# Sums of attention weights in one PSUM bank, and new positions for every task of a fused attention and soft mixture-of-experts kernel

## The chip, the cores and the metric

One NeuronCore of a Trainium2 chip runs the whole program. The metric is the device time of one execution in microseconds; lower is better. All data is float32 in and out.

## The reference, cut to what matters

```
# q, k, v: (8 batches, 8 heads, 576 positions, 64)
q_rot, k_rot = (rotate(q), rotate(k))              # halves mixed by cos and sin of the position
scores = scale * np.matmul(q_rot, k_rot.transpose(0, 1, 3, 2))
scores = scores - np.max(scores, axis=-1, keepdims=True)
attn = np.exp(scores)
attn = attn / (np.sum(attn, axis=-1, keepdims=True) + 1e-09)
x = np.matmul(attn, v)                             # -> (4608 tokens, 512)

logits = x @ phi                                   # phi: (512, 32 slots)
d = softmax of logits over all tokens ; slot_input = d.T @ x
slot_out[e] = np.maximum(slot_input[e] @ w1[e], 0.0) @ w2[e]     # 8 experts, 4 slots each
c = softmax of logits over the slots ; out = c @ slot_out
```

Both softmaxes subtract a maximum and add 1e-9 to the sum that they divide by. The four lines on the experts are cut; the first six are as they stand in the reference.

## The kernel before, in words

Two heads make a pair; there are 32 pairs, four to a batch. A pair keeps head 0 in partitions 0 to 63 and head 1 in 64 to 127, with the position (576, worked on as two halves of 288) along the free axis. After the last pair comes a tail: the slots, the experts' two layers with 64 weight tiles of 512 KB, and the output.

What one pair goes through, by task name:

- `load0`, `load1`: q and k by DMA into one of two buffers `x_in`. `spin0`, `spin1`: GpSimd multiplies them by cos and sin in place, four pieces of 128x288 each. `join`: VectorE adds the two products. `high0`, `high1`: ScalarE casts to float16. `low`: VectorE takes what the cast lost; both go into `hl`, and `x_in` is free for the next pair but one.
- `m00` to `m31` and `m_rem`: nine times TensorE makes a block of the scores in plain float16 and VectorE reduces it to a negated maximum `nm` (L175, L183). `m_min`, `m_turn`, `m_half`, `m_rows`: the maxima are joined, transposed, scaled and sent by DMA into a row `peak`.
- `t0` to `t8`: TensorE makes the scores, keys along the partitions, with three float16 products and a fourth that subtracts the maximum (16 matmuls, L220); ScalarE writes exp of them to SBUF (L221). Two of `t0` to `t7` share a tile `a_t` of 128x1152, of which there are four; `t8` writes `a_rem`. The sum over the keys is thus a sum over partitions and over nine pieces.
- `av0` to `av8`: TensorE multiplies the weights by v (8 instructions, L236) into one PSUM tile; `o_out` copies it to `xt` on ScalarE (L244).
- `add1`, `add2`, `add3`: VectorE adds the four tiles `a_t` into `c_t`: two additions of 128x1152 (L253) and one of 128x576 (L255). `total`: TensorE sums four pieces over the partitions with a matrix `pick` of ones and zeros (16 instructions, L265), each piece in an own 32 columns of the array, the two halves of the positions in two banks. `total_out` copies the sums to SBUF on ScalarE (L270).
- `send`: four DMAs lay the sums out over 96 partitions (`rc`, L276). `recip`: VectorE adds the four and takes the reciprocal (L282, L283). `spread`, `widen`: two steps of DMA through DRAM spread it over all partitions (`rb`, L289, L296). `norm`: GpSimd multiplies `xt` (L299). The last two pairs do this by TensorE and VectorE instead (`sums_turn`, `sums_wide`, `norm_wide`).
- `logits`, `logits_sum`, `natural`, `natural_out`: the pair's part of the logits, and `xt` transposed. After every fourth pair come `stats` and `step`: the running softmax over tokens, `slot_input`, and the softmax over slots.

TensorE writes everything but the products with v into tiles `s_ps` of two banks each, of which there are three, taken in turn. Each engine, and the DMA queue of SyncE (SP), carries out its instructions in the order in which they are written. That order is set by the table `WHEN`: a task's number is its place in a cycle of four units, counted from the pair's own cycle, and all pairs use the same numbers. So a pair's load stands four cycles ahead of its `t0`, and its `natural` nearly three cycles behind. The start, up to the first `t0`, is written out by hand (lines 600 to 660). While pairs run, `weights` loads 25 weight tiles, one in a cycle; `trickle` loads eight more once the buffers of q and k are free.

Of the kernel before, what the change touches and what calls it, by code (L numbers as in the profile page):

```python
# [7 lines left out]
F32 = mybir.dt.float32  # L8
# [39 lines left out]
    "load0": -15.9, "load1": -14.496, "spin0": -13.466, "spin1": -12.4, "join": -9.9, "high0": -9.4817, "high1":  # L48
    -9.0595, "low": -8.0, "m01": -6.5262, "m10": -5.894, "m00": -5.0601, "m11": -4.7, "load_v": -3.85, "m20": -3.771,
    "m21": -3.317, "m30": -2.9, "m31": -2.7, "m_rem": -2.6642, "m_min": -2.49, "m_turn": -1.744, "m_half": -1.667,  # L50
# [4 lines left out]
    "o_out": 4.52, "add3": 4.6009, "total": 5.54, "total_out": 5.55, "send": 5.56, "sums_turn": 6.0, "sums_wide": 6.3,  # L55
    "norm_wide": 6.4, "logits_late": 7.0, "logits_sum_late": 7.05, "recip": 7.294, "natural_late": 7.3, "spread": 7.31,
    "natural_out_late": 7.35, "widen": 7.3768, "norm": 8.706, "logits": 10.54, "logits_sum": 10.579, "stats": 11.3708,
    "natural": 11.52, "natural_out": 11.536,
}
QL, QH, KH, KL = range(4)  # L60
# [3 lines left out]
def attn_softmoe(ctx, tc, qk, v, phi, w1, w2, cs, ident, sel, seg, out):  # L64
# [30 lines left out]
    bits = const.tile([P, 5], F32, name="bits")  # L95
    ones, warm, tiny, fold = bits[:, 0:1], bits[:, 1:2], bits[:, 2:3], bits[:, 3:5]
# [8 lines left out]
    pick = const.tile([P, NS + 1], F32, name="pick")  # L105
    nc.gpsimd.memset(pick, 0.0)
    for h in (0, 1, 2):
        nc.gpsimd.memset(pick[rows[h % 2], h:h + 1], 1.0)

    nc.vector.memset(tiny, 0.0)  # L110
    nc.vector.memset(tiny[0:32], 1e-9)
# [146 lines left out]
    rcs = [const.tile([96, 4, RC], F32, name=f"rc{i}") for i in range(2)]  # L258
# [27 lines left out]
    def spread(p, eng):  # L286
        rr = sg.pop(p)
        rd = dram.tile([2, S], F32, name="r_row")
# [645 lines left out]
```

## Time and profile before

| | |
|---|---|
| median of 3 runs | 613.8 us (610.75 to 618.16) |
| span of the profiled execution | 611.8 us |
| busy: TensorE, VectorE | 532.9 us (87%), 497.0 us (81%) |
| busy: ScalarE, GpSimd | 326.9 us (53%), 315.1 us (52%) |
| DMA | 111.63 MB, 182 GB/s over the span |
| first and last `o_out` | 49.9 and 525.6 us from the span's start |

The span runs from the first to the last instruction of the profiled execution; its own device time is not given apart from it, and the span lies 2.0 us below the median of the runs, within their spread. The pairs take the stretch from 50 to 526 us, the tail the rest.

### The profile page before, as it was taken

The page shows a single profiled execution, that of the slowest core. Times are in us where ns is not written, and L with a number is a line of the kernel's source. Part 1 is how long each engine was busy: PE and PEld are TensorE (multiplying, and loading weights), DVE is VectorE, ACT ScalarE, POOL GpSimd, SP SyncE. Part 2 cuts the span into 40 slices and gives each one's busy share as a digit, 9 for nine tenths or more (in the row PEclk, how much of TensorE's full clock was granted, in tenths as well). Part 3 has the DMA queues.
Part 4 walks back from the last instruction along what each step waited for, and adds up shares of the span by engine and source line. Part 5 has one row for each costly group of instructions (what it writes and reads, how often), then busy time and mean ns, then how long its engine had stood idle before and what let it go on. Part 6 is the DMA issues. An engine that isn't in the chain of part 4 may idle for free.

```text
span 611.8 us, 23277 instructions
## 1 busy us (share of the span) xinstructions
PE 532.9 (87%) x10064; PEld 352.1 (58%) x10064; DVE 497.0 (81%) x729; ACT 326.9 (53%) x647; POOL 315.1 (52%) x308
## 2 busy tenths in 40 slices
PE   3668999998999899989999899898898999799981
PEld 2346666656765566666656565666566666443551
DVE  6879899999998999999998999999899874322341
ACT  2145656665665565656656566565465655324441
POOL 2668498655676566647763857658654000100000
PEclk9679999999999999999999999999899999859996
DMA  7153555555555555555555555455542246649999
GB/s 260 60 195 119 175 174 173 174 174 173 174 173 174 174 174 174 173 175 174 174 173 175 173 174 174 174 174 174 171 141 62 64 130 206 206 142 350 349 376 298
DMA packets 71734, 111.63 MB, mean 182 GB/s; under 512 B 20176, under 2 KB 47568, under 8 KB 71632
## 3 DMA queue, kind: packets, MB, share of 16 engines
q1 hardware_dynamic: 71618, 110.15, 54.5%
q8 instruction: 79, 1.29, 0.9%
q14 instruction: 23, 0.19, 0.1%
q10 hardware_dynamic: 14, 0.00, 0.0%
HBM read 99.93 MB, written 9.58 MB: 179 GB/s over the span
## 4 chain that ended last, share of the span: by engine, by line
PE 35%; DVE 26%; DMA 20%; ACT 6%; SPq 5%; issue 5%; POOL 1%; DVEq 0%; ACTq 0%
PE s_ps L220 8%; PE o_ps L236 8%; DVE nm L175 7%; DMA rc<-s 7%; DMA w_exp<-in_w 6%; DVE c_t L253 6%; DVE hl L153 5%; SPq L276 4%; ACT a_t L221 3%; PE s_ps L265 3%; DMA x_in<-in_qk 3%; PE s_ps L773 3%; DMA v_in<-in_v 2%; DVE c_t L255 2%; PE s_ps L173 2%
## 5 line engine op out<-in xcount | busy, mean ns | idle before, releaser
L140 POOL TENSOR_TENSOR x_in<-x_in,cs_sb 128x288 f32<-128x288 f32 x248 | 264.9, 1101 | 63.0 <-DMA x_in<-in_qk 38.1
L221 ACT ACTIVATE a_t<-s_ps 128x576 f32<-128x576 f32 x256 | 158.9, 649 | 97.8 <-PE s_ps L220 95.9
L175 DVE TENSOR_REDUCE nm<-s_ps 128x2 f32<-128x576 f32 x256 | 187.1, 743 | 15.1 <-PE s_ps L173 14.9
L236 PE MATMUL o_ps<-a_t,v_in 64*64 64x288 f32 x2048 | 172.4, 413 | 1.0 <-ACT xt L244 0.3
L220 PE MATMUL s_ps<-hl 64*64 64x288 f16 x3456 | 155.5, 286 | 16.4 <-DVE nm L175 15.9
L220 PEld LDWEIGHTS <-hl 64*64 64x64 f16 x3456 | 104.4, 107 | 59.9 <-issue 43.8
L299 POOL TENSOR_TENSOR xt<-xt,rb 128x576 f32<-128x576 f32 x30 | 42.8, 1425 | 141.0 <-DMA rb<-r_row 104.1
L173 PE MATMUL s_ps<-hl 64*64 64x288 f16 x1024 | 82.1, 298 | 26.0 <-DVE nm L175 20.5
L220 PE MATMUL s_ps<-peak,lift 64*64 64x288 f16 x1152 | 89.1, 284 | 0.0
L236 PEld LDWEIGHTS o_ps<-a_t,v_in 64*64 64x64 f32 x2048 | 72.9, 133 | 21.0 <-issue 7.3
L173 PEld LDWEIGHTS <-hl 64*64 64x64 f16 x1024 | 45.0, 107 | 49.1 <-issue 37.7
L149 ACT CAST hl<-x_in 128x576 f16<-128x576 f32 (+1 forms) x66 | 40.1, 650 | 33.1 <-DVE x_in L144 30.3
L270 ACT ACTIVATE s<-s_ps,bits 128x576 f32<-128x576 f32 x32 | 23.7, 740 | 58.0 <-PE s_ps L265 26.3
L144 DVE TENSOR_TENSOR x_in<-x_in 128x1152 f32<-128x1152 f32 (+2 forms) x36 | 53.4, 1483 | 0.5 <-POOL x_in L140 0.4
L253 DVE TENSOR_TENSOR c_t<-c_t,a_t 128x1152 f32<-128x1152 f32 x32 | 51.6, 1611 | 0.0
L153 DVE TENSOR_TENSOR hl<-x_in,hl 128x1152 f16<-128x1152 f32 x32 | 49.5, 1546 | 1.8 <-ACT hl L149 1.8
L253 DVE TENSOR_TENSOR c_t<-a_t 128x1152 f32<-128x1152 f32 x32 | 50.6, 1582 | 0.0
L220 PEld LDWEIGHTS <-lift 64*64 64x64 f16 x1152 | 38.1, 108 | 0.6
L265 PE MATMUL s_ps<-c_t,pick 128*32 128x288 f32 x256 | 37.1, 411 | 0.0
L265 PE MATMUL s_ps<-a_rem,pick 128*32 128x288 f32 x128 | 36.9, 411 | 0.0
L265 PE MATMUL s_ps<-a_t,pick 128*32 128x288 f32 x128 | 36.9, 411 | 0.0
L221 ACT ACTIVATE a_rem<-s_ps 128x576 f32<-128x576 f32 x32 | 20.8, 651 | 17.0 <-PE s_ps L220 17.0
(183 smaller groups left out, 597.6 us busy)
## 6 DMA issues: line engine op xcount, KB each, us to landing
x_in<-in_qk SPq DMA_DIRECT2D x62, 576.0 KB
w_exp<-in_w SPq DMA_DIRECT2D x63, 512.0 KB
v_in<-in_v SPq DMA_DIRECT2D x32, 576.0 KB
rb<-r_row SPq DMA_DIRECT2D x60, 144.0 KB
out<-w_exp SPq DMA_DIRECT2D x16, 512.0 KB
rc<-s SPq DMA_DIRECT2D x120, 4.5 KB
x_in<-in_qk SPq DMA_DIRECT2D x4, 288.0 KB
out<-w_exp SPq DMA_DIRECT2D x4, 256.0 KB
```

The costliest lines, as they stand in the source:

```text
L140: eng.tensor_tensor(out=x[:, :, c], in0=x[:, :, c], in1=cs_sb[:, :, c], op=ALU.mult)
L144: nc.vector.tensor_tensor(out=x[:, t, 0, c], in0=x[:, t, 0, c], in1=x[:, t, 1, c], op=ALU.add)
L149: nc.scalar.copy(out=halves[p][:, 1 + t, c], in_=loaded[p][:, t, 0, c])
L153: nc.vector.tensor_tensor(out=hl[:, 0:4:3], in0=x[:, :, 0], in1=hl[:, 1:3], op=ALU.subtract)
L173: nc.tensor.matmul(s[rows[c], h, 0:HC], lhsT=hl[rows[h], QH, at:at + D], rhs=hl[rows[h], KH, half[n]], start=True, stop=True)
L175: nc.vector.tensor_reduce(out=nms[p][:, n, j:8:4], in_=s[:, :, 0:HC], axis=AX.X, op=ALU.max, negate=True)
L220: nc.tensor.matmul(s[rows[h ^ n], n, 0:HC], lhsT=lhs, rhs=rhs, start=(i == 0), stop=(i == 3))
L221: nc.scalar.activation(out=weights_of(p, b).rearrange("p (n x) -> p n x", n=2), in_=s[:, :, 0:HC], func=AF.Exp, scale=SCALE)
L236: nc.tensor.matmul(o[rows[h], n, 0:HC], lhsT=vt[r, b, n], rhs=a[r, half[n]], start=(b == 0), stop=(b == KB - 1))
L253: nc.vector.tensor_tensor(out=c, in0=c if j > 1 else ats[p, 0], in1=a, op=ALU.add)
L265: nc.tensor.matmul(s[32 * i:32 * i + 32, n, 0:HC], lhsT=pick[:, n:n + NS], rhs=m[:, half[n]], start=True, stop=True, tile_position=(0, 32 ...
L299: eng.tensor_tensor(out=xts[p], in0=xts[p], in1=rbs.pop(p), op=ALU.mult)
```

## The change

The weights of `t4` to `t7` are no longer all added on VectorE. `add1` is as before; `add2` now adds only the first half of the third `a_t` (128x576), and `add3` is gone. `total` sums six pieces in place of four, in three rounds that accumulate in PSUM; the two halves of the positions take 32 columns of the array each, so the result fills 288 columns of one bank in place of two times 288. `total_out` then copies 128x288, `send` is two DMAs, `recip` adds two parts, `widen` reads rows of 288 in place of 576. The sums' other readers (`sums_turn`, `sums_wide`, `norm_wide`) follow that layout.

The table of positions has one number for each pair's place in its batch, and a table of its own (`FIRST`) for the first four pairs; the start, the steps after each batch and the last pairs are in tables too, and all tasks are sorted by them. With that the order of nearly all tasks of all engines differs, at the start also of the loads of q, k, v, `ident` and `phi`. The small matrix `fold` is made by one GpSimd addition late in the run instead of four VectorE copies at the start. The last 64 of the 576 positions are transposed as columns 448 to 576 and used from partitions 64 to 127.

```diff
 WHEN = {
-    "load0": -15.9, "load1": -14.496, "spin0": -13.466, "spin1": -12.4, "join": -9.9, "high0": -9.4817, "high1":
...
+    "load0": (-16.4019, -15.2769, -15.1452, -14.3382), "load1": (-14.3952, -13.4352, -13.0199, -13.9565), "spin0":
...
+FIRST = {
+    "load0": (-16.6363, -9.672, -3.3892, -0.9218), "load1": (3.3939, -6.7488, -2.9737, -0.5436), "spin0": (-7.8087,
...
     def add(p, j):
         if j == 1:
             cts[p] = att.tile([P, 2, S], F32, name="c_t")
-        c, a = cts[p], ats[p, j]
-        if j < 3:
-            nc.vector.tensor_tensor(out=c, in0=c if j > 1 else ats[p, 0], in1=a, op=ALU.add)
+            nc.vector.tensor_tensor(out=cts[p], in0=ats[p, 0], in1=ats[p, 1], op=ALU.add)
         else:
-            nc.vector.tensor_tensor(out=c[:, 1], in0=c[:, 1], in1=a[:, 1], op=ALU.add)
+            c = cts[p][:, 0]
+            nc.vector.tensor_tensor(out=c, in0=c, in1=ats[p, 2][:, 0], op=ALU.add)
...
     def total(p):
-        c, r, a = cts.pop(p), rems[p], ats[p, 3]
+        c, a2, a3 = cts.pop(p), ats[p, 2], ats[p, 3]
+        streams = ((c[:, 0], c[:, 1], a2[:, 1]), (a3[:, 0], a3[:, 1], rems[p]))
         sg[p] = s = bank2()
-        for n in range(2):
-            for i, m in enumerate((c[:, 0], c[:, 1], r, a[:, 0])):
-                nc.tensor.matmul(s[32 * i:32 * i + 32, n, 0:HC], lhsT=pick[:, n:n + NS], rhs=m[:, half[n]],
-                                 start=True, stop=True, tile_position=(0, 32 * i))
+        for i in range(3):
+            for k in range(2):
+                for n in range(2):
+                    g = 32 * (n + 2 * k)
+                    nc.tensor.matmul(s[g:g + 32, 0, 0:HC], lhsT=pick[:, 16 * n:16 * n + 32], rhs=streams[k][i][:, half[n]],
+                                     start=(i == 0), stop=(i == 2), tile_position=(0, g))
 
     def total_out(p):
-        s, s4 = sg[p], late.tile([P, S], F32, name="s4", bufs=1)
-        nc.scalar.activation(out=s4.rearrange("p (n x) -> p n x", n=2), in_=s[:, :, 0:HC], func=AF.Identity, bias=tiny)
+        s, s4 = sg[p], late.tile([P, HC], F32, name="s4", bufs=1)
+        nc.scalar.activation(out=s4, in_=s[:, 0, 0:HC], func=AF.Identity, bias=tiny)
         sg[p] = s4
 
     def send(p, eng):
         s4, rc = sg.pop(p), rcs[p % 2]
-        for i in range(4):
-            eng.dma_start(out=rc[:, i, :], in_=s4[32 * i:32 * i + 2])
+        for k in range(2):
+            eng.dma_start(out=rc[:, k, :], in_=s4[64 * k:64 * k + 64:16])
...
+    def folds():
+        nc.gpsimd.tensor_tensor(out=fold, in0=id_sb[:, 0:64:16], in1=id_sb[:, 64:128:16], op=ALU.add)
...
-    nc.vector.memset(fold, 0.0)
-    for i in range(0, P, 32):
-        nc.vector.tensor_copy(out=fold[i:i + 2], in_=id_sb[i:i + 2, i:i + 2])
...
+    tasks = [(at, name, 0) for name, at in ONCE.items()]
+    for name, at in WHEN.items():
+        last = NPAIR - 2 if name in SLOW else NPAIR
+        tasks.extend((FIRST[name][p] if p < NP else 4 * p + at[p % NP], name, p) for p in range(last))
...
+    for at, name, p in sorted(tasks):
+        if at < 4 * NPAIR or p < NPAIR - 1:
+            do(name, p)
```

In the pairs 12 to 15 the new tables give, for example, this order around one `total` (VectorE's tasks among them): `m31.13 t3.12 m_rem.13 av1.12 m01.14 total.11 total_out.11 m_min.13 join.15 t4.12 high0.15 av2.12 m10.14 t5.12 add1.12 t6.12 av3.12 logits.10`; the old table gives `m31.15 m_rem.15 av1.14 m01.16 m_min.15 total.13 total_out.13 t4.14 t5.14 join.17 m10.16 av2.14 m_turn.15 m_half.15 high0.17 logits.12 logits_sum.12 add1.14 m00.16`.

## Rows read from the trace of the kernel before

**Rows 1.** The page: span, then busy time by engine, share of the span, instructions.

```profile
span 611.8 us, 23277 instructions
PE 532.9 (87%) x10064; PEld 352.1 (58%) x10064; DVE 497.0 (81%) x729; ACT 326.9 (53%) x647; POOL 315.1 (52%) x308
```

**Rows 2.** Window of the tail: length, busy us by engine, granted clock, DMA share, GB/s.

```profile
540.00:612.00 72.00, 55.53 (x510) 28.56 (x510) 20.78 (x38) 26.29 (x55) 2.59 (x3) 0.86 0.97 320
```

**Rows 3.** The line of o_out, with first and last start.

```profile
L244 ACT COPY xt<-o_ps x32: 637/638/640, 49.9 to 525.6; 128x576 f32<-128x576 f32 x32
```

**Rows 4.** Windows of twelve pairs, 184.8 to 370.5 us: length, busy us by engine.

```profile
sum 185.70, PE 170.28 PEld 116.16 DVE 175.59 ACT 112.04 POOL 120.54; mean PE 56.76 PEld 38.72 DVE 58.53 ACT 37.35 POOL 40.18
```

**Rows 5.** Waits in those twelve pairs: us in total, times, longest; SP's own last.

```profile
PE s_ps L173 <- DVE nm L175: 6.6, 7, 1.8
PE s_ps L220 <- DVE nm L175: 5.0, 13, 0.6
SPq L276 <- ACT a_t L221: 59.2, 12, 7.2
```

**Rows 6.** Groups of VectorE in those twelve pairs: busy us, mean ns.

```profile
L253 DVE TENSOR_TENSOR c_t<-c_t,a_t 128x1152 f32<-128x1152 f32 x13 | 22.3, 1719 | 0.0
L255 DVE TENSOR_TENSOR c_t<-c_t,a_t 128x576 f32<-128x576 f32 x12 | 8.9, 744 | 0.0
```

**Rows 7.** Windows of one late pair: all engines; then TensorE's line L220 alone.

```profile
495.20:510.00 14.80, 14.67 (x301) 9.63 (x304) 8.88 (x16) 8.42 (x20) 1.52 (x2) 1.00 0.49 152
...
495.20:510.00 14.80, 5.90 (x156) 1.00 0.49 152
```

**Rows 8.** Groups of TensorE in that late pair.

```profile
L173 PE MATMUL s_ps<-hl 64*64 64x288 f16 x12 | 1.0, 294 | 0.1
...
L181 PE MATMUL s_ps<-hl 64*64 64x288 f16 x4 | 0.4, 283 | 0.0
```

**Rows 9.** Timeline of TensorE in that late pair: start, length, instruction.

```profile
494.86 0.33 PE L387 MATMUL s_ps<-id_sb,d_t 128*128 128x128 f32 x1
...
495.40 0.32 PE L173 MATMUL s_ps<-hl 64*64 64x288 f16 x4
495.52 0.56 PE L220 MATMUL s_ps<-hl 64*64 64x288 f16 x12
...
498.32 0.42 PE L395 MATMUL s_ps<-xn,dn 64*32 64x128 f32 x8
...
499.56 0.41 PE L265 MATMUL s_ps<-c_t,pick 128*32 128x288 f32 x2
...
499.80 0.41 PE L265 MATMUL s_ps<-c_t,pick 128*32 128x288 f32 x2
...
500.64 0.56 PE L220 MATMUL s_ps<-hl 64*64 64x288 f16 x12
...
504.49 0.33 PE L408 MATMUL s_ps<-id_sb,l_sb 128*128 128x128 f32 x1
...
504.86 0.72 PE L236 MATMUL o_ps<-a_t,v_in 64*64 64x288 f32 x8
...
508.20 0.55 PE L220 MATMUL s_ps<-hl 64*64 64x288 f16 x12
...
508.69 0.67 PE L236 MATMUL o_ps<-a_t,v_in 64*64 64x288 f32 x8
```

**Rows 10.** Timeline of weight loads in the same total.

```profile
499.56 0.12 PEld L265 LDWEIGHTS s_ps<-c_t,pick 128*32 128x32 f32 x2 [0.30 <-issue]
```

**Rows 11.** Timeline of VectorE at the start.

```profile
13.11 2.86 DVE L630 COPY bits<-id_sb 2x2 f32<-2x2 f32 x4
16.00 4.08 DVE L175 TENSOR_REDUCE nm<-s_ps 128x2 f32<-128x576 f32 x6
```

**Rows 12.** Groups of ScalarE by line and shape, whole span.

```profile
L270 ACT ACTIVATE s<-s_ps,bits 128x576 f32<-128x576 f32 x32 | 23.7, 740 | 58.0 <-PE s_ps L265 26.3 <-DMA w_exp<-in_w 15.5 <-DMA v_in<-in_v 11.5
```

**Rows 13.** The waits over the whole span: us in total, times, longest.

```profile
POOL xt L299 <- DMA rb<-r_row: 104.1, 24, 14.3
```

More of the change, by code (lines that the diff above doesn't have):

```diff
@@ new lines @@
+    3.6811), "o_out": (4.8784, 4.7532, 4.6296, 4.2983), "total": (5.7529, 5.5594, 5.1412, 4.9378), "total_out":
+    (5.8475, 5.7089, 5.282, 4.971), "send": (6.4739, 6.3131, 6.1856, 5.6953), "recip": (6.8303, 6.8467, 7.2922,
+    6.5543), "spread": (7.8252, 7.2981, 7.5691, 7.5261), "widen": (8.6569, 8.8329, 7.6411, 8.2716), "norm": (9.2243,
+    9.0042, 9.5345, 9.5602), "logits": (10.4353, 9.7107, 10.2396, 10.2058), "logits_sum": (10.5697, 9.8766, 10.3288,
+    10.6509), "natural": (11.7335, 11.2387, 10.7192, 10.5465), "natural_out": (11.8374, 11.81, 10.9117, 10.6927),
+}
@@ new lines @@
+FIRST = {
[7 rows of a table added]
+    0.9797, 4.8955), "m_min": (-1.8161, 0.2847, 3.8164, 8.985), "m_turn": (-1.5365, 0.9973, 4.608, 9.0201),
+    "m_half": (-1.1633, 1.3076, 4.7158, 9.1675), "m_rows": (-0.9042, 1.3412, 4.8956, 9.7967), "t0": (-0.5942, 2.274,
[10 rows of a table added]
+    "total": (3.5342, 6.9553, 11.83, 16.8974), "total_out": (3.7547, 7.3464, 12.3148, 17.3476), "send": (4.6646,
+    8.2796, 13.747, 18.0924), "recip": (4.7894, 9.0523, 14.1035, 18.907), "spread": (5.6109, 9.0962, 15.1044,
+    19.1915), "widen": (7.9783, 10.1227, 15.6861, 19.2354), "norm": (9.6721, 12.3981, 16.9174, 21.0434), "logits":
+    (10.7374, 13.6624, 18.3509, 22.3911), "logits_sum": (11.4538, 14.2347, 18.4316, 22.4255), "natural": (9.7991,
+    13.7893, 19.0161, 22.7323), "natural_out": (10.0259, 14.4457, 19.1548, 22.7891),
+}
@@ L60 @@
+SLOW = ("send", "recip", "spread", "widen", "norm", "logits", "logits_sum", "natural", "natural_out")
 QL, QH, KH, KL = range(4)
@@ L540, in fast, with end, run @@
-    def fast(task):
-        return lambda p: p >= NPAIR - 2 and task(p)
-    plan = {
-        "load0": lambda p: fetch(p, 0),
-        "load1": lambda p: fetch(p, 1),
-        "spin0": lambda p: spin(p, 0, nc.gpsimd, parts),
-        "spin1": lambda p: spin(p, 1, nc.gpsimd, parts),
-        "join": join,
-        "high0": lambda p: high(p, 0),
-        "high1": lambda p: high(p, 1),
+    ends = {}
+    def end(name):
+        def run(p):
+            if p not in ends:
+                ends[p] = {"stat": stat_tasks(p // NP), "comb": c_soft_tasks(p // NP)}
+            if name == "slot" and name not in ends[p]:
+                ends[p]["slot"] = slot_tasks(p // NP)
+            next(ends[p][name], None)
+        return run
@@ new lines, in rest, with begin_load, begin_spin @@
+    def rest(begin, task):
+        return lambda p: task(p) if p else begin()
+    def begin_load():
+        load(0)
+        for t, cc in ((1, 0), (1, 1), (0, 0), (0, 1)):
+            c = half[cc]
+            if t:
+                nc.sync.dma_start(out=cs_sb[:, :, c], in_=cs[:, :, c])
+            nc.sync.dma_start(out=loaded[0][:, t, :, c], in_=qk[0, t][:, :, c])
+    def begin_spin(t):
+        for c in half:
+            spin(0, t, nc.vector, (c,))
+            join(0, t, c)
+            high(0, t, c)
@@ new lines, in heat, with tables, skip @@
+    def heat(n):
+        o = bank2()
+        for i in range(n):
+            nc.tensor.matmul(o[:, 0, 0:HC], lhsT=lift, rhs=halves[0][:, KH, 0:HC], start=True, stop=True)
+    def tables():
+        nc.sync.dma_start(out=phi_sb, in_=phi.rearrange("(c p) n -> p c n", p=P))
+        nc.sync.dma_start(out=sel_sb, in_=sel)
+    def folds():
+        nc.gpsimd.tensor_tensor(out=fold, in0=id_sb[:, 0:64:16], in1=id_sb[:, 64:128:16], op=ALU.add)
+    def skip():
+        pass
+    plan = {
+        "load0": rest(begin_load, lambda p: fetch(p, 0)),
+        "load1": rest(skip, lambda p: fetch(p, 1)),
+        "spin0": rest(lambda: begin_spin(0), lambda p: spin(p, 0, nc.gpsimd, parts)),
+        "spin1": rest(lambda: begin_spin(1), lambda p: spin(p, 1, nc.gpsimd, parts)),
+        "join": lambda p: p > 1 and join(p),
+        "join0": lambda p: join(1, 0),
+        "join1": lambda p: join(1, 1),
+        "high0": rest(skip, lambda p: high(p, 0)),
+        "high1": rest(skip, lambda p: high(p, 1)),
@@ L593, in do @@
     def do(name, p):
-        if (name, p) not in done and 0 <= p < NPAIR:
+        if (name, p) not in done:
             done.add((name, p))
             plan[name](p)
-    beat = sorted((when % 4, int(when // 4), name) for name, when in WHEN.items())
-    load(0)
-    for t, cc in ((1, 0), (1, 1), (0, 0), (0, 1)):
-        c = half[cc]
-        if t:
-            nc.sync.dma_start(out=cs_sb[:, :, c], in_=cs[:, :, c])
-        nc.sync.dma_start(out=loaded[0][:, t, :, c], in_=qk[0, t][:, :, c])
@@ L606, in attn_softmoe @@
-    do("load0", 1)
-    do("load1", 1)
-    nc.sync.dma_start(out=id_sb, in_=ident)
-    do("load_v", 0)
-    for t in (1, 0):
-        for c in half:
-            spin(0, t, nc.vector, (c,))
-            join(0, t, c)
-            high(0, t, c)
-    o = bank2()
-    def heat(n):
-        for i in range(n):
-            nc.tensor.matmul(o[:, 0, 0:HC], lhsT=lift, rhs=halves[0][:, KH, 0:HC], start=True, stop=True)
-    heat(N_WARM)
-    low(0)
-    done.update((n, 0) for n in ("spin0", "spin1", "join", "high0", "high1", "low", "load0", "load1"))
@@ L670, in attn_softmoe @@
         trickle(p)
-    while pending:
-        step(p)
     release_stk()
-    for name in ("add1", "add2", "av4", "av5", "add3", "av6", "av7", "av8", "o_out", "total", "total_out"):
+    for name in ("add1", "add2", "av4", "av5", "av6", "av7", "av8", "o_out", "total", "total_out"):
         do(name, p)
```

201 lines of the change are left out of this document (86 added, 115 removed), and 35 rows, old and new, of tables (FIRST, WHEN).

## The prediction

> **What bounds the kernel now.** I read the page first: TensorE is busy for 87% of the span and VectorE for 81% [rows 1], which names two suspects and no winner, since the share mixes the pairs with the tail. So next the windows by stage. In the tail the DMA engines are 97% busy [rows 2]; nothing of this change makes the tail's transfers fewer, and its length counts from the end of the pairs. The pairs are the stage to look at: the first and the last `o_out` start at 49.9 and 525.6 us [rows 3], 31 steps of 15.35 us.
>
> In a quiet stretch of twelve pairs (15.48 us each) VectorE is busy for 175.59 of 185.70 us, 94.6%, or 14.63 us a pair; TensorE for 170.28, or 14.19 us; ScalarE for 9.34 and GpSimd for 10.05 us [rows 4]. So VectorE has the least room. TensorE stands idle for 15.4 us of that stretch, and the view of waits gives 11.6 us of it to one cause, a PSUM tile that VectorE has not yet reduced [rows 5]. With three such tiles and every engine in fixed order, TensorE fills the tiles, then waits until VectorE comes out of a long addition. VectorE sets the pace, and TensorE is close behind it.
>
> How close, a busy share can't say, because the modelled ends of matmuls count as busy while nothing follows them. The last pairs say it. They have few maxima left to reduce; in one of them VectorE is busy for only 8.88 of 14.80 us and TensorE for 14.67 [rows 7]: that is TensorE at its own pace. The stretch holds 156 instructions of L220, 9.75 tasks of 16 where a pair has 9, and four blocks of maxima where a pair has nine (three of L173, one of L181) [rows 7, 8]. A block takes 0.12 us of the queue and a task of scores 0.49 [rows 9]. A whole pair of that kind thus needs 14.80 + 5 x 0.12 - 0.75 x 0.49 = 15.03 us. In it is the work that comes once in four pairs: 494.86 to 495.40, 498.32 to 499.56 and 504.49 to 504.86, together 2.15 us [rows 9]. A mean pair needs 15.03 - 2.15 + 2.15/4 = 13.42 us of TensorE. The other 2.06 us of the 15.48 are waits, seen or hidden in such ends.
>
> **The change, part by part.** VectorE loses `add3` (744 ns), and `add2` shrinks from 128x1152 (1719 ns) to the shape that `add3` had (744 ns) [rows 6]. Together 744 + 1719 - 744 = 1719 ns go: 14.63 - 1.72 = 12.91 us a pair are left. All of it lay on the engine that sets the pace.
>
> TensorE gains a third round in `total`. Now two rounds, eight groups of four instructions each in an own quarter of the columns taken two passes at a time, go from 499.56 to 500.64, and one step from a group to the next is 0.24 us [rows 9]. A round is two steps, 0.48 us. Its accumulation in place needs no other engine. No row shows six streams into one bank; from below, a cost under zero is excluded, since eight instructions are added and none is removed; from above I take the load of weights unhidden. For that the trace has a row: the loads of the next group start at 499.56, with the matmuls, and take 0.12 us beside them [rows 10]. Eight of them on the path would add 0.96 us. I take 0.48 us, since the steps of 0.24 us have such loads inside them. TensorE's own need becomes 13.42 + 0.48 = 13.90 us.
>
> The Trainium skill has a rule against this part: "TensorE: Matmul & The Clock Gate", Part 3 (The mechanism), says that a weight load runs beside matmuls in flight only when its group of rows differs, and all streams of `total` use the same rows. By it each added stream would pay its load. The trace does not agree, with loads and matmuls of the same rows at 499.56; the rule stays as a rival below.
>
> Off the path, each with its cover: `total_out` copies half of 740 ns [rows 12] on an engine that is 60% busy; without that cover it would be a gain of 0.3 us a pair at most. `send` is two DMAs less on SP's queue, which now stands 4.9 us a pair at `send` waiting for ScalarE [rows 5] with the loads of v, of q and k behind it; the wait belongs to `total_out`, so what is behind gains little. `widen` reads twice as many runs half as long; what waits for it is `norm`, where GpSimd sits idle for 104.1 us over the span [rows 13] and has a third of its time free. At nothing, then, and if that room were gone some tenths of a microsecond a pair. The fold on GpSimd comes once. The transposes of the last 64 positions keep their number.
>
> The new positions can't be costed from rows one by one, as an order that has not run leaves none. What can be read is the order itself, shown ahead. In the new one VectorE has, from `m01` on, two reductions with `join` between them until the tile of `m10` is free: twice 0.68 us (six took 4.08 [rows 11]) and a long addition, by the 1.72 us of [rows 6], 3.1 us. TensorE has `total`, three tasks of scores and the block of `m10` before `logits` wants that tile, 1.56 + 3 x 0.49 + 0.12 = 3.15 us, and two `av` besides: covered. In the old order it had `total`, two tasks of scores and the block, 1.08 + 2 x 0.49 + 0.12 = 2.18 us, with one `av`, `m_turn` and `logits` besides: barely. On SP the two loads of a pair now stand one behind the other's `weights` and `send`, so the second can come a third of a cycle later; their buffer still comes free nearly two cycles before `join` needs the data. So I let the positions remove waits and add none; the ends are all of the 2.06 us and none.
>
> At the start the four copies for `fold`, 2.86 us, stand directly ahead of the first reductions, and these begin as the copies end [rows 11]. They leave VectorE; the identity matrix now lands behind the second load of pair 2, but it is first wanted at the transpose of the maxima, after nine reductions. I take 2.9 us for the start, with ends of zero (another chain, GpSimd's of pair 1, is as late) and 6 us.
>
> **The sum.** How much of the 2.06 us of waits stays? With VectorE at 60% nearly none [rows 7], at 94.6% all. At 12.91 us of work in a cycle of 14.6 it is busy for 88%. I take a third, 0.7 us, because waiting behind a queue falls much faster than the load: a pair takes 13.90 + 0.70 = 14.60 us, 0.88 less. Of the 31 steps the last three are TensorE's own already and get 0.48 us longer. So 28 x -0.88 = -24.6, 3 x 0.48 = +1.4, the start -2.9: together -26.1 us. The span of 611.8 us becomes 585.7. It lies 2.0 us below the median of the runs, and I put the same sum against the median: 587.7, say 588 us.
>
> **The rivals.**
>
> *TensorE is fed without a gap.* Positions and lighter VectorE leave 0.1 us of waits: 14.0 us a pair, 28 x -1.48 + 1.4 - 2.9 = -42.9, 571 us. For it speaks the late pair with its 0.13 us of idle time; against it that there VectorE had 40% free.
>
> *The waits fall only as VectorE's load does.* In a straight line between 60% and 94.6%: with 12.91 us of work the cycle that agrees with itself is 15.33 us (84% busy, 1.43 us of waits). 28 x -0.15 + 1.4 - 2.9 = -5.7, 608 us. For it: the long additions `join`, `low` and `add1` are still there, and it is they, not the mean load, that hold the tiles.
>
> *The added streams pay their weight loads.* 14.60 + 0.96 = 15.56 us a pair, +0.08; 28 x 0.08 + 3 x 1.44 - 2.9 = +3.6, 617 us. It is what the Trainium skill's rule above would do here. Against it stands the row of the loads.
>
> *Slower: the waits are the tiles', not VectorE's.* If three PSUM tiles in turn cost TensorE its 2.06 us whatever VectorE does, TensorE becomes the bound and pays its third round in full: 13.90 + 2.06 = 15.96, 28 x 0.48 + 1.4 - 2.9 = +11.9, 626 us. It decides from 1.63 us of remaining waits on, where the start's gain is eaten too. Against it: 11.6 of 15.4 idle us end at a reduction by VectorE. New positions that leave a buffer or a load late would look the same and are in this case's chance.
>
> **How the numbers follow.** Forecast 0.48; fed without a gap 0.20; as the load does 0.19; weight loads 0.05; slower 0.08. 1% either way, 6 us, is about what a measurement of this kernel can tell, its three runs being 7 us apart. From 571 to 608 us the first three cases reach, and with the start's ends I put the range at 568 to 609; what is left out is the last two cases and the tips of the others. Faster by over 1% (below 607.7): the forecast, the first rival and a little over half of the second, 0.79. Slower by over 1%: 0.09. The rest, 0.12, within.
>
> **What would show it.** Twelve quiet pairs should take about 175 us, with VectorE busy for 155 (88%) and TensorE idle for less than 10; the group of L253 on `c_t` alone should have half its work in 128x576 at 744 ns; `total` should go from its first matmul to the next task in 1.56 us, steps of 0.24. The first reduction should start near 13 us, the first `o_out` near 47. The prediction is wrong if the waits of TensorE on the reductions stay above 1 us a pair, if a step of `total` is longer than 0.24 us, or if VectorE itself waits, on `rc` before `recip` or on GpSimd before `join`.

## The result, and the profile after

The changed kernel takes 583.15 us (median of 4 runs, 577.06 to 587.93), the kernel before 612.27 us beside it. Forecast were 588 us, range 568 to 609. The ratio is 0.945, 95% interval 0.9369 to 0.9531; here and in the table below it leaves out executions over 1.5% above the fastest of their kernel (586.39 and 587.93 us here), so that it stands for some 34 us where the medians are 29.1 us apart. The profile is of the execution of 586.39 us (span 584.6), called the longer one; a repetition (e8 below) left one of 581.91 us (span 580.1), the shorter one, and where the two differ the text says from which a row is.

The page of the changed kernel answers to [rows 1]:

```profile
span 584.6 us, 23522 instructions
PE 526.7 (90%) x10320; PEld 355.2 (61%) x10320; DVE 439.8 (75%) x690; ACT 322.1 (55%) x647; POOL 299.7 (51%) x309
```

VectorE fell from 497.0 to 439.8 us; 57.2 us over 32 pairs is 1.79 us a pair. TensorE has 256 instructions more, 8 a pair, and in the twelve pairs below it is now the fullest engine.

Twelve quiet pairs, from the start of the tenth `o_out` to that of the 22nd, as in [rows 4]; columns are length, then busy us of each engine (with instructions), granted clock, DMA share, GB/s. First the longer, then the shorter execution:

```profile
172.00:351.20 179.20, 168.79 (x3644) 117.40 (x3637) 154.08 (x238) 109.71 (x223) 111.08 (x111) 1.00 0.57 177
```

```profile
171.50:346.20 174.70, 168.90 (x3645) 117.84 (x3638) 154.84 (x238) 109.62 (x223) 111.39 (x111) 1.00 0.57 182
```

In the shorter one a pair takes 14.56 us, VectorE is busy for 88.6% and TensorE idle for 5.8 us: nearly what was forecast (175 us, 88%, under 10). The longer one does the same work in 4.5 us more, and all of that is idle time of TensorE (10.4 us). One and the same kernel thus has 14.93 and 14.56 us a pair; a smaller difference between two profiles says nothing by itself. What TensorE waits for in the longer one, over the same twelve pairs (us in total, times, longest):

```profile
PE s_ps L406 <- POOL xt L356: 8.9, 6, 2.7
PE s_ps L274 <- DVE nm L229: 0.4, 1, 0.4
PE s_ps L274 <- DVE nm L237: 0.2, 1, 0.2
```

The waits on VectorE's reductions, 11.6 us in [rows 5], are down to 0.6. In their place stands a wait that the kernel before did not have: `logits` (L406) for `xt`, which GpSimd's `norm` (L356) has not written yet. `norm` itself waits for `widen`. In the shorter execution it is less:

```profile
PE s_ps L406 <- POOL xt L356: 3.4, 3, 1.9
```

Groups of VectorE in the same stretch of the longer execution: busy us, mean ns of one, idle before it with its releaser:

```profile
L198 DVE TENSOR_TENSOR x_in<-x_in 128x1152 f32<-128x1152 f32 x12 | 17.2, 1435 | 0.0
L305 DVE TENSOR_TENSOR c_t<-a_t 128x1152 f32<-128x1152 f32 x12 | 16.7, 1388 | 0.0
L308 DVE TENSOR_TENSOR c_t<-c_t,a_t 128x576 f32<-128x576 f32 x12 | 10.5, 878 | 0.0
...
L338 DVE TENSOR_REDUCE rr<-rc 96x12 f32<-96x24 f32 x12 | 2.0, 166 | 0.4 <-DMA rc<-s 0.4
```

The reader sees `add2` (L308) in half its shape, `add3` gone, and neither of the waits that would have made the prediction wrong: `join` (L198) doesn't wait for GpSimd, `recip` (L338) for 0.4 us in all.

`total` in the timeline of TensorE, shorter execution (start, length, instruction), answers to [rows 9]:

```profile
189.23 0.44 PE L321 MATMUL s_ps<-c_t,pick 128*32 128x288 f32 x2
...
189.49 0.41 PE L321 MATMUL s_ps<-c_t,pick 128*32 128x288 f32 x2
...
189.74 0.41 PE L321 MATMUL s_ps<-c_t,pick 128*32 128x288 f32 x2
...
189.98 0.41 PE L321 MATMUL s_ps<-c_t,pick 128*32 128x288 f32 x2
...
190.23 0.41 PE L321 MATMUL s_ps<-a_rem,pick 128*32 128x288 f32 x2
190.46 0.41 PE L321 MATMUL s_ps<-a_t,pick 128*32 128x288 f32 x2
...
190.82 0.32 PE L227 MATMUL s_ps<-hl 64*64 64x288 f16 x4
```

Six groups, from 189.23 to 190.46 in five steps of 0.23 to 0.26 us, and the next task 1.59 us after the first matmul; 1.56 was forecast. Three of the steps are 0.01 or 0.02 us over the 0.24 above which the prediction was to count as wrong; their mean is 0.25. The `total` of [rows 9] goes on at 500.04 and 500.29, so its steps are 0.24 and 0.25 too: the step has not grown, the limit had no room.

The start in VectorE's timeline answers to [rows 11], and the line of `o_out` to [rows 3]:

```profile
11.32 1.73 DVE L207 TENSOR_TENSOR hl<-x_in,hl 128x1152 f16<-128x1152 f32 x1 [0.50 <-ACT hl L203]
12.98 4.07 DVE L229 TENSOR_REDUCE nm<-s_ps 128x2 f32<-128x576 f32 x6
```

```profile
L298 ACT COPY xt<-o_ps x32: 632/639/642, 43.5 to 500.2; 128x576 f32<-128x576 f32 x32
```

The reductions follow `low` directly, at 12.98 in place of 16.00 us. So the time before was 49.9 us to the first `o_out`, 475.7 to the last and 86.2 of tail; it is now 43.5, 456.7 and 84.4, and in the shorter execution 44.6, 451.6 and 83.9.

### The profile page after: what moved, and what is told of

It reads as the page before. It is cut to its first block, busy times and chain, and to the rows that moved or that the text cites. A ratio compares the mean times of both kernels' runs of the same rounds, so it can differ in the third digit from the quotient of the medians.

```text
span 584.6 us, 23522 instructions
## 1 busy us (share of the span) xinstructions
PE 526.7 (90%) x10320; PEld 355.2 (61%) x10320; DVE 439.8 (75%) x690; ACT 322.1 (55%) x647; POOL 299.7 (51%) x309
## 4 chain that ended last, share of the span: by engine, by line
PE 47%; DMA 16%; DVE 15%; POOL 4%; issue 3%; ACT 3%; SPq 2%; POOLq 0%; ACTq 0%; DVEq 0%
PE o_ps L290 12%; PE s_ps L274 10%; DMA rb<-r_row 8%; PE s_ps L321 5%; DVE nm L229 5%; DMA r_row<-rr 4%; DVE hl L207 3%; PE s_ps L227 3%; POOL xt L356 3%; PE s_ps L803 3%; PE s_ps L406 2%; PE s_ps L392 2%; DVE c_t L308 2%; DVE c_t L305 2%; DMA w_exp<-in_w 1%
## 5 line engine op out<-in xcount | busy, mean ns | idle before, releaser
L194 POOL TENSOR_TENSOR x_in<-x_in,cs_sb 128x288 f32<-128x288 f32 x248 | 245.3, 1022 | 77.9 <-DMA x_in<-in_qk 65.3
L229 DVE TENSOR_REDUCE nm<-s_ps 128x2 f32<-128x576 f32 x256 | 185.7, 750 | 35.7 <-PE s_ps L227 33.5
L274 PEld LDWEIGHTS <-hl 64*64 64x64 f16 x3456 | 108.6, 108 | 34.8 <-issue 10.5
L356 POOL TENSOR_TENSOR xt<-xt,rb 128x576 f32<-128x576 f32 x30 | 46.0, 1534 | 114.8 <-DMA rb<-r_row 85.0
L321 PE MATMUL s_ps<-a_t,pick 128*32 128x288 f32 x384 | 52.2, 409 | 0.0
L326 ACT ACTIVATE s<-s_ps,bits 128x288 f32<-128x288 f32 x32 | 16.0, 501 | 65.5 <-issue 29.7
L203 ACT CAST hl<-x_in 128x576 f16<-128x576 f32 (+1 forms) x66 | 42.4, 661 | 16.8 <-DVE x_in L198 16.3
L207 DVE TENSOR_TENSOR hl<-x_in,hl 128x1152 f16<-128x1152 f32 x32 | 51.3, 1602 | 0.5 <-ACT hl L203 0.5
L198 DVE TENSOR_TENSOR x_in<-x_in 128x1152 f32<-128x1152 f32 (+2 forms) x36 | 47.5, 1319 | 0.3 <-POOL x_in L194 0.2
L305 DVE TENSOR_TENSOR c_t<-a_t 128x1152 f32<-128x1152 f32 x32 | 45.6, 1424 | 0.0
L406 PE MATMUL s_ps<-xt,phi_sb 128*32 128x128 f32 x256 | 13.6, 284 | 18.9 <-POOL xt L356 17.4
L237 DVE TENSOR_REDUCE nm<-s_ps 128x2 f32<-128x576 f32 x32 | 24.1, 752 | 5.8 <-PE s_ps L235 5.8
L308 DVE TENSOR_TENSOR c_t<-c_t,a_t 128x576 f32<-128x576 f32 x32 | 27.5, 860 | 0.2
```

The source lines that it names most:

```text
L194: eng.tensor_tensor(out=x[:, :, c], in0=x[:, :, c], in1=cs_sb[:, :, c], op=ALU.mult)
L198: nc.vector.tensor_tensor(out=x[:, t, 0, c], in0=x[:, t, 0, c], in1=x[:, t, 1, c], op=ALU.add)
L203: nc.scalar.copy(out=halves[p][:, 1 + t, c], in_=loaded[p][:, t, 0, c])
L207: nc.vector.tensor_tensor(out=hl[:, 0:4:3], in0=x[:, :, 0], in1=hl[:, 1:3], op=ALU.subtract)
L229: nc.vector.tensor_reduce(out=nms[p][:, n, j:8:4], in_=s[:, :, 0:HC], axis=AX.X, op=ALU.max, negate=True)
L274: nc.tensor.matmul(s[rows[h ^ n], n, 0:HC], lhsT=lhs, rhs=rhs, start=(i == 0), stop=(i == 3))
```

## The experiments

Theory: VectorE's order of tasks made TensorE wait, and the shorter additions took most of those waits away, while the third round costs TensorE its 0.48 us. Rivals: the new positions did it, not the additions; TensorE alone is the bound by now; the rest is held by a third thing. Each run below stands against the kernel before on its own chip; "pair" is the mean of the twelve quiet pairs of its profiled execution.

| run | median, us (range) | ratio, 95% interval | pair, us | first `o_out` |
|---|---|---|---|---|
| the changed kernel, first profile | 583.15 (577.06 to 587.93) | 0.9369 to 0.9531 | 14.93 | 43.5 |
| e8 the changed kernel again | 583.47 (577.75 to 587.86) | 0.9434 to 0.9558 | 14.56 | 44.6 |
| e1 old order, new sums | 605.9 (600.95 to 607.08) | 0.9763 to 0.9898 | 15.08 | 52.8 |
| e2 new order, old sums | 632.56 (624.24 to 638.1) | 1.0091 to 1.0295 | 16.11 | 44.7 |
| e6 copies at the start | 586.92 (584.91 to 593.38) | 0.9534 to 0.9605 | 14.86 | 46.9 |
| e4 a fourth round | 590.19 (588.05 to 590.98) | 0.9532 to 0.9658 | 14.81 | 42.7 |
| e5 one addition more | 608.98 (607.14 to 615.81) | 0.9911 to 0.9993 | 15.64 | 44.5 |
| e9 no `add2` | 581.41 (574.33 to 584.26) | 0.9332 to 0.9485 | 14.61 | 43.0 |
| e10 two rounds | 578.28 (576.51 to 584.03) | 0.935 to 0.9496 | 14.84 | 43.8 |
| e3 sums first on SP | 590.85 (590.26 to 592.81) | 0.9553 to 0.9661 | 15.01 | 44.4 |
| e7 sums and loads | 595.13 (593.78 to 596.13) | 0.9686 to 0.9747 | 15.21 | 44.9 |
| e11 no load delayed | 576.49 (574.6 to 578.22) | 0.9319 to 0.9413 | 14.58 | 43.3 |
| e12 e9, e10 and e11 together | 571.86 (570.76 to 578.16) | 0.9256 to 0.9352 | 14.58 | 45.5 |

**The same kernel again.** e8 is the changed kernel without an edit.

> The changed kernel unchanged, for a second profile beside the others of this set: 577 to 588 us, the same waits of logits on norm in two of four kinds of pair.

Its profile is the shorter execution used above: 0.4 us of TensorE's waits in the twelve pairs are left to reductions, and the wait of `logits` makes the difference between these two executions.

**The two halves of the change.** e1 is the kernel before, its order and its start, with the six streams:

```diff
-    "o_out": 4.52, "add3": 4.6009, "total": 5.54, "total_out": 5.55, "send": 5.56, "sums_turn": 6.0, "sums_wide": 6.3,
+    "o_out": 4.52, "total": 5.54, "total_out": 5.55, "send": 5.56, "sums_turn": 6.0, "sums_wide": 6.3,
...
-            nc.vector.tensor_tensor(out=c[:, 1], in0=c[:, 1], in1=a[:, 1], op=ALU.add)
+            c = cts[p][:, 0]
+            nc.vector.tensor_tensor(out=c, in0=c, in1=ats[p, 2][:, 0], op=ALU.add)
```

> The old order of all tasks with the new sums: add3 gone, add2 halved, three rounds in total. If the arithmetic carries the gain (VectorE loses 1.72 us a pair, TensorE pays 0.48), twelve quiet pairs fall from 185.7 to 180 us or less and the time to 596 to 602 us, with the start unchanged at 49.9 us. If the positions carry it, the old order, made around the longer additions, keeps its waits and pays the third round: 608 to 622 us.

e2 is the changed kernel with the additions, `total` and the layout of the sums as before, and places for `add3`:

```diff
+WHEN["add3"] = (4.628, 4.5986, 3.4273, 3.5)
...
+FIRST["add3"] = (2.8662, 6.5396, 10.2634, 14.9531)
```

> The new order with the old sums: add2 over 128x1152, add3 (placed right behind add2), two rounds in total, four DMAs in send. If the arithmetic carries the gain, VectorE stays the bound at 14.6 us of work a pair, quiet pairs stay at 15.2 to 15.5 us and only the start's 6.4 us come off: 602 to 608 us. If the positions carry it, pairs fall to 14.9 us as in the changed kernel: 583 to 592 us.

The windows of the twelve quiet pairs, e1 and then e2, with e2's two largest waits of TensorE:

```profile
184.60:365.50 180.90, 173.71 (x3637) 118.60 (x3637) 164.82 (x238) 110.32 (x224) 118.96 (x110) 1.00 0.52 176
```

```profile
188.50:381.80 193.30, 170.80 (x3549) 115.71 (x3542) 173.31 (x250) 113.31 (x222) 123.14 (x112) 0.97 0.52 165
```

```profile
PE s_ps L276 <- DVE nm L231: 11.4, 9, 2.3
PE s_ps L404 <- POOL xt L355: 5.8, 3, 1.9
```

The arithmetic alone brings 0.40 us a pair and 8 us in all by the medians (10 by the ratio); the new order alone, with `add3` where e2 puts it, makes the kernel slower. Under the old additions the new order has the old waits on the reductions, and the granted clock drops to 0.97. So neither "the additions did it" nor "the positions did it" holds: the order is one for the short additions, and the gain of 29 us is that of both together. The wait of `logits` for `xt`, on the other hand, comes with the order: e2 has it, e1 has none of it in its twelve pairs. So does the shorter start: 44.7 us in e2, 52.8 in e1.

**The start.** e6 puts four copies of the old kind and a memset back ahead of the first reductions:

```diff
+    def begin_low():
+        low(0)
+        scratch = const.tile([P, 2], F32, name="scratch")
+        nc.vector.memset(scratch, 0.0)
+        for i in range(0, P, 32):
+            nc.vector.tensor_copy(out=scratch[i:i + 2], in_=pick[i:i + 2, i // 4:i // 4 + 2])
...
-        "low": low,
+        "low": rest(begin_low, low),
```

> The changed kernel with a memset and four small VectorE copies back ahead of the first reductions, as they stood before (2.9 us). If that part of the start is on the path, the first o_out is 2.5 to 3.5 us later than in the changed kernel and so is the end. If GpSimd's products of pair 1 or the loads are as late, under 1 us, and the new order of the start gives its whole 6.4 us.

Its timeline of VectorE:

```profile
14.01 2.79 DVE L627 COPY scratch<-pick 2x2 f32<-2x2 f32 x4
16.84 2.75 DVE L229 TENSOR_REDUCE nm<-s_ps 128x2 f32<-128x576 f32 x4
```

The reductions are back at 16.84 us, but the first `o_out` comes at 46.9, not 49.9: against the mean of 43.5 and 44.6 the copies are worth 2.9 us, as a rough size, since the other runs with the new order spread from 42.7 to 45.5. The other 3.0 of the 5.9 us came with the order. With it came another granted clock: from 13 to 40 us, a mixture of the levels 2.4 and 1.2 GHz, it is 0.68 of full speed in the kernel before and in e1, 0.81 in e8, e2 and e6, and 0.87 in the longer execution of the changed kernel. What is the order's and what the clock's was not told apart, nor why e1 is 2.9 us later than the kernel before, whose start it has.

**More work on one engine.** e4 gives `total` a fourth round, which repeats the third one's streams; e5 gives VectorE one more operation of 128x576 behind `add2`, a maximum that leaves the values as they are:

```diff
-        for i in range(3):
+        for i in range(4):
...
+            nc.vector.tensor_tensor(out=c, in0=c, in1=ats[p, 2][:, 0], op=ALU.max)
```

> The changed kernel with a fourth round in total that counts the third round's pieces again, so its sums are larger than the reference's. If TensorE sets the pace of the pairs now, each pair pays the 0.48 us: 15 us more than the changed kernel, 596 to 600 us. If something off TensorE sets it (the sums' way through the DMAs), less than 6 us more: 583 to 589 us. If weight loads are not hidden, a round is longer than 0.48 us by up to 0.96: over 610 us.

> The changed kernel with one more VectorE instruction of 128x576 behind add2 (a maximum that changes no value), 0.74 to 0.88 us a pair, as long as the add3 that went. If VectorE no longer sets the pace, at most 5 us more than the changed kernel of the same set. If it still does, 0.74 us x 28 pairs or more: over 20 us more, near 604 us.

The windows of the twelve pairs, e4, then e5 with what TensorE waits for:

```profile
173.00:350.70 177.70, 173.57 (x3740) 120.44 (x3733) 154.33 (x238) 109.46 (x222) 110.18 (x111) 1.00 0.56 179
```

```profile
178.60:366.30 187.70, 171.38 (x3644) 118.36 (x3637) 170.22 (x250) 109.87 (x223) 121.53 (x111) 0.99 0.54 169
```

```profile
PE s_ps L274 <- DVE nm L229: 7.6, 6, 2.5
PE s_ps L393 <- DVE nm L229: 3.5, 3, 1.3
```

The fourth round takes as long as the third: from the first matmul of `total` to the next task it is 1.11 us in the kernel before, 1.59 in the changed one and 2.08 in e4 (medians of the 32 pairs). These 0.48 us more of TensorE cost 7 us against e8, about half of the 15 us expected if every pair paid them and a little more than the 6 us of the other case; the intervals of the two ratios overlap by 0.0026, and the 0.25 us more a pair are less than the two executions of the changed kernel differ by. One short operation more on VectorE cost 25 us and 1.08 us a pair, and brought back 11.1 us of waits on the reductions. TensorE at 97% of busy time has some room left, VectorE at 89% hardly any: e5 is the clearest run for the theory.

**Less work on one engine.** e9 leaves out `add2`, e10 the second of three rounds:

```diff
-            c = cts[p][:, 0]
-            nc.vector.tensor_tensor(out=c, in0=c, in1=ats[p, 2][:, 0], op=ALU.add)
+            pass
...
-        for i in range(3):
+        for i in (0, 2):
```

> The changed kernel without add2: the first half of the third tile of weights is left out of the sums. VectorE has one addition of 128x576 (0.75 to 0.9 us) less per pair, TensorE the same. If the order of VectorE's tasks still sets the pace, twelve quiet pairs fall from 174.7 us to about 165 to 168 (13.8 to 14.0 us a pair) and the time by 15 to 20 us. If TensorE alone is the bound by now, as its 97% of busy time suggests, the pairs stay within 0.1 us of 14.56 and the time falls by 3 us at most.

> The changed kernel without the second of the three rounds of total: the second half of c_t and of the sums' fourth tile is left out of the sums. TensorE has 8 instructions, 0.48 us by the steps of 0.24, less per pair, VectorE the same. If TensorE alone is the bound, a pair falls by all of it to 14.1 us and the time by 13 to 15 us. If VectorE's order sets the pace, a pair falls by 0.2 us at most and the time by at most 6 us, as adding a round cost only 0.26 us a pair.

e9's window and its only large wait of TensorE, then e10's window and its two:

```profile
168.30:343.60 175.30, 167.68 (x3642) 117.41 (x3638) 144.73 (x226) 109.93 (x222) 107.17 (x113) 1.00 0.57 181
```

```profile
PE s_ps L405 <- POOL xt L355: 6.5, 5, 1.9
```

```profile
168.70:346.80 178.10, 165.88 (x3549) 115.04 (x3542) 155.30 (x239) 110.18 (x223) 114.93 (x113) 0.99 0.57 178
```

```profile
PE s_ps L406 <- POOL xt L356: 6.5, 4, 1.9
PE s_ps L274 <- DVE nm L229: 2.5, 3, 1.0
```

Here my theory in its simple form fell. With 0.84 us less a pair (10.1 us over the twelve), VectorE hardly makes TensorE wait any more, and yet the pair is no shorter; the medians of e9 and e10 are 2 and 5 us below that of e8, inside ranges that overlap. In e10 TensorE has 3.0 us less work than in the shorter execution of the changed kernel and is idle for 12.2 us, where that one has 5.8 and the longer one 10.4: what was taken from it turned into waiting. Relief of either engine alone doesn't shorten the pair, as far as these profiles can tell. In both runs what ends TensorE's largest waits is `norm`, late with `xt`.

**The wait for `xt`.** `spread` and `widen` pass the reciprocals through DRAM, on SP's queue, among the loads. SP in the changed kernel, longer and then shorter execution (issue, length, instruction):

```profile
241.09 0.40 SPq L189 DMA_DIRECT2D x_in<-in_qk  x1
242.19 0.34 SPq L345 DMA_DIRECT2D r_row<-rr  x1
242.57 0.43 SPq L540 DMA_DIRECT2D w_exp<-in_w  x1
248.36 1.31 SPq L352 DMA_DIRECT2D rb<-r_row  x2
```

```profile
238.53 0.40 SPq L189 DMA_DIRECT2D x_in<-in_qk  x1
240.97 0.34 SPq L345 DMA_DIRECT2D r_row<-rr  x1
241.36 0.43 SPq L540 DMA_DIRECT2D w_exp<-in_w  x1
242.48 1.31 SPq L352 DMA_DIRECT2D rb<-r_row  x2
```

The same four instructions: `spread` (L345, 4.5 KB) is issued 1.1 us behind a load of 576 KB in the one and 2.4 us behind it in the other, and `widen` (L352), which needs its data, follows after 6.2 and 1.5 us. These are the ends of a spread: at the other places of this kind in the twelve pairs, with the load 1.1 to 1.5 us ahead, it follows after 3.85 and 3.60 us in the longer execution and after 4.28 and 4.03 in the shorter one. What the DMA engines moved in 40 slices from 240 to 250 us of the longer execution:

```profile
GB/s 5 0 66 0 8 0 1 0 147 166 221 332 442 406 461 176 97 102 181 254 328 393 377 213 107 8 0 0 9 8 16 8 25 25 25 16 0 0 0 124
```

From the ninth value to the 25th, 242.0 to 246.25 us, the two loads move, with `spread` issued between them; `widen` is released 2.1 us after the last of it.

That `norm` waits for these transfers is not new: GpSimd waits for `rb` 40.1 us in the twelve pairs of the kernel before, 36.0 and 33.7 us in the two executions of the changed one. New is how close `logits` follows. In the old table `norm` stands at 8.706 and `logits` at 10.54, in the new one at 9.00 to 9.56 and at 9.71 to 10.44. That this shorter distance makes the wait is a reading of the tables; no run changes it alone.

Two orders were to take the sums' transfers out from between the loads (six or seven numbers of `WHEN`; the lines that differ):

```diff
+for name, kind, at in (("load_v", 3, -3.33), ("widen", 1, 7.31), ("load1", 2, -12.67), ("send", 2, 5.29),
+                       ("recip", 2, 6.6), ("spread", 2, 6.61), ("widen", 2, 6.62)):
+    WHEN[name] = WHEN[name][:kind] + (at,) + WHEN[name][kind + 1:]
```

That is e3; e7 has `load1` at -15.14, ahead of those transfers, and is the same otherwise.

> The changed kernel with seven positions moved, so that spread and widen (in one kind of pair also send and recip) come on SP ahead of the loads that now stand between them. If the logits wait for norm because the sums' small DMAs stand behind large loads, TensorE's idle time before logits falls from 0.9 to under 0.3 us a pair and the time to 562 to 570 us. The rival, that TensorE's waits only move to another place once logits is served: 578 to 586 us, with TensorE idle as long before other tasks.

> As the run that put the sums' DMAs first on SP, but the one load of k that it pushed behind widen, and for which GpSimd then stood still, now goes directly behind the load of q, ahead of all of them. If the logits wait for norm because of what stands between the small DMAs, logits waits under 3 us in twelve quiet pairs and the time is 8 to 16 us below the changed kernel of the same set. If another wait takes its place again, within 4 us of the changed kernel.

GpSimd's wait for the loads of q and k over twelve pairs, in the changed kernel (longer execution) and e3:

```profile
POOL x_in L194 <- DMA x_in<-in_qk: 19.4, 10, 3.3
```

```profile
POOL x_in L197 <- DMA x_in<-in_qk: 55.2, 15, 10.6
```

The largest wait of TensorE, e3 and then e7:

```profile
PE s_ps L409 <- POOL xt L359: 8.6, 3, 3.0
```

```profile
PE s_ps L277 <- DMA peak<-mr: 8.8, 3, 3.4
```

Both orders made it slower, and neither came out as one of its two expectations. With `send` at 5.29 SP stands there until ScalarE has copied the sums (51.3 and 52.7 us of the twelve pairs, against 27.0 in the longer execution of the changed kernel), and the loads of q and k are behind it. GpSimd then waits for `x_in`, up to 10.6 us at a time in e3 and 10.5 in e7. In e3 `logits` still waits for `xt`. In e7 it doesn't, and the time is 12 us above e8 all the same: `t0` waits for the row of maxima, `peak`, instead. The wait had changed its place.

e11 moves no load of q and k, and `send` less far:

```diff
+for name, kind, at in (("load_v", 3, -3.33), ("widen", 1, 7.31), ("send", 2, 6.045),
+                       ("recip", 2, 6.85), ("spread", 2, 6.86), ("widen", 2, 7.59)):
+    WHEN[name] = WHEN[name][:kind] + (at,) + WHEN[name][kind + 1:]
```

> The changed kernel with six numbers changed for SP, so that the small transfers of the sums (spread, widen) are not issued among the loads of q, k and weights that follow, and no load of q and k is put behind a wait it did not have. If the wait of logits for xt is those transfers landing late, it falls from 8.9 us (3.4 us in the better execution) to under 3 us in twelve pairs, the time comes to 575 to 579 us and the executions lie closer together. If SP's waits only change places, as in the two earlier orders, another wait grows and the time is 582 us or more.

Its window, what TensorE waits for most, and GpSimd's wait for the loads:

```profile
167.80:342.80 175.00, 169.15 (x3645) 117.84 (x3638) 154.96 (x239) 109.64 (x223) 111.34 (x112) 1.00 0.55 181
```

```profile
PE s_ps L277 <- DMA peak<-mr: 3.1, 3, 1.6
POOL x_in L197 <- DMA x_in<-in_qk: 51.9, 16, 6.0
```

In these pairs the wait of `logits` for `xt` is gone (over the whole span 3.7 us are left, where the changed kernel has 17.4 and 12.2), and where `spread` follows a load after 1.04 us, now with no load issued for 4 us behind it, `widen` comes 2.9 to 3.4 us later. The time is 576.49 us with 3.6 us between the fastest and the slowest of four executions, where the changed kernel's eight have 10.9. Its interval lies below that of e8 and overlaps the first one's by 0.0044, so it is some 1% better, not more. GpSimd waits for its loads nearly as long in all as in e3, but at most 6.0 us at a time; so the sum of that wait does not explain why e3 and e7 were slower, and whether its longest pieces do was not tried. The quiet pairs of e11 are no shorter than those of the shorter execution of the changed kernel: a new wait stands where the old one was, `t0` for the row of maxima (`peak`), a small transfer on the same queue. What e11 removes looks like the late case, not a part of every pair; its profile is of its fastest execution, and its longer ones left none.

**Both engines less, and that order.**

> The three last edits together: SP's six new numbers, no add2, and total without its second round. Left out of the sums are the first half of the third tile of weights and the second halves of c_t and of the fourth tile. Alone, less work on VectorE brought 2 us and less on TensorE 5 us, though adding as much to VectorE had cost 25. If the two engines bind together, so that relief of one only meets the other, relief of both frees the pair: about 0.5 us less, 14.1 us, and 560 to 567 us beside the 576.5 us of the six numbers alone. If a third thing holds the pairs by now (SP's transfers, the products p of the chain from the sums to logits, the fixed places of the tiles), the time stays within 4 us of that, 572 us or more.

Its window and its waits of TensorE (this profile is of the longest of five executions, 578.16 us; the other four lie between 570.76 and 572.40):

```profile
170.50:345.40 174.90, 164.81 (x3546) 114.67 (x3541) 145.54 (x226) 110.36 (x222) 109.41 (x112) 1.00 0.55 182
```

```profile
PE s_ps L277 <- DMA peak<-mr: 2.7, 2, 1.9
PE s_ps L394 <- DVE nm L232: 2.0, 2, 1.2
PE s_ps L251 <- DVE nm L244: 2.0, 2, 1.2
```

The median is 4.6 us below that of e11, between the two expectations and nearer the second; the intervals of the two ratios overlap by 0.0033. Relief of both engines at once is not the sum that would come of two engines in balance. TensorE is idle for 10.1 us, in small pieces with several causes: `peak`, the tile of the transposes `natural` (L394), the reduction in `m_min` ahead of `m_turn` (L251). What keeps the pairs at 14.6 us is thus neither of the two engines' work; the written order, with SP's small transfers in it, is what is left. That is an argument and not shown, and which link of it comes first is open.

## Why the prediction was right, step by step

**VectorE's relief** is right: 14.63 - 1.72 = 12.91 us a pair forecast, 154.84 / 12 = 12.90 measured. Part of the exact fit is luck: `add2` takes 852 ns (878 in the longer execution), not the 744 of [rows 6], `join` takes 1437 ns where it took 1660 in the kernel before, and the twelve pairs of [rows 6] hold 13 of the long `add2`, so that 14.63 is a little high for one pair.

**TensorE's own need**, 13.90 us, is right within 0.1 us or so: e9, where VectorE doesn't hold it, has 167.68 / 12 = 13.97 us of busy time, the changed kernel 14.07, with some waiting hidden in modelled ends. The third round goes in steps of 0.25 us, as read (the eight groups of four in the prediction are four groups of four, and the steps are right), and e4 suggests that another one is not even paid in full. The rival of the unhidden weight loads, 617 us, falls with it. The rule of the Trainium skill that it came from ("TensorE: Matmul & The Clock Gate", Part 3, The mechanism: a load of weights runs beside matmuls in flight only if its group of rows is another) does not agree with these rows, in which all streams use the same 128 rows of the array and different columns.

**The waits** came out at the forecast size for another reason. "A third of 2.06 us stays", 0.70 us, was said of waits behind VectorE's queue. In the shorter execution the idle time of TensorE is 5.8 / 12 = 0.48 us a pair, but of the waits on reductions only 0.4 / 12 = 0.03 us is left. VectorE's share vanished, as in the rival "fed without a gap", and the wait for `xt` took its place. The transfers of the sums had been costed at nothing, as GpSimd sits idle before `norm` anyway. That cover was there for `norm`, but in the new order not for `logits` behind it. That the pair came out within 0.04 us of the 14.60 forecast is luck; in the longer execution it is 14.93. e5 shows the mechanism of the forecast all the same: waits fall much faster than the load. At 12.90 us of work they are 0.03 us a pair; in e5, at 170.22 / 12 = 14.19, they are 11.1 / 12 = 0.93 us, and the straight line of the second rival (608 us) is out.

**"Positions remove waits and add none"** is the step that failed, though it cost little. The short additions need them (e1 without them brings 8 of the 29 us), and without the short additions they make the kernel slower (e2). And they do add a wait, that for `xt`: 8.9 us of twelve pairs in the longer execution, 3.4 in the shorter one.

**The sum.** Forecast: 28 steps by -0.88, -24.6; last three +1.4; start -2.9; tail nothing. Measured between the `o_out` of the shorter and the longer execution: 28 steps -27.1 and -20.8; last three +3.0 and +1.8; start -5.3 and -6.4; tail -2.3 and -1.8. The mean of the two is -29.5 us, 3.4 more than the -26.1 forecast. The 28 steps lie on both sides of the forecast; the terms that were too small are the start and the tail, and the last three steps cost 1 us more than forecast. At the start the forecast had only the copies, which e6 puts at about 2.9 us; as much again came with the order, with the clock in it. The bound of 6 us had it in. The median has moved by 29.1 us; by the ratios it is 34 us and, in e8, 31.

**The slower rival**, that three tiles cost TensorE its 2.06 us whatever VectorE does, is ruled out by 0.03 us a pair of remaining waits on them (0.05 in the longer execution).

## What to carry to other kernels

When the fullest engine is relieved, ask not only what the next engine needs, but which small transfer has been hidden behind the old wait: a step that was costed at nothing because its own engine idles can still hold the one that reads its result. An order written out by hand fits one set of durations; try the arithmetic and the order apart before crediting either, and don't expect that taking work away brings what adding the same work costs: on VectorE the one brought 2 us here and the other cost 25. When small transfers are moved away from the large ones on a load queue, look at what waits behind them afterwards; two of three such orders here cost more than they brought.

## What the runs showed of the hardware

A transfer of 4.5 KB took 1.5 us until its reader was issued when the large load ahead of it was issued 2.4 us earlier, with another load 0.4 us behind it; it took 3.6 to 6.2 us when the load ahead was issued 1.1 to 1.5 us earlier and the next 0.4 us behind, and 2.9 to 3.4 us when the load ahead was 1.04 us earlier and none followed for 4 us (e11).

The tail got shorter although the experts' loads and matmuls, which fill most of it, are as before. Its first 25 us in the kernel before, the changed kernel and e11 (the eighth column is the granted clock):

```profile
525.60:550.60 25.00, 21.25 (x158) 11.00 (x154) 7.02 (x22) 7.10 (x19) 3.53 (x8) 0.66 0.62 197
```

```profile
500.20:525.20 25.00, 20.98 (x178) 10.31 (x170) 6.88 (x21) 9.48 (x24) 3.56 (x8) 0.80 0.55 186
```

```profile
490.30:515.30 25.00, 20.98 (x204) 10.45 (x200) 8.42 (x25) 10.83 (x28) 4.40 (x9) 0.93 0.66 216
```

The granted clock is 0.66, 0.80 and 0.93 of full speed, a mixture of the levels 2.4 and 1.2 GHz, and the tails are 86.2, 84.4 and 82.5 us long. TensorE's busy time is nearly the same, in which it carries out 158, 178 and 204 instructions. The clock is not the whole of it: e1 has 0.80 in the same stretch, as the changed kernel, and a tail of 86.8 us. What makes the clock fall for longer in one kernel than in another was not tried.
